# A PSUM tile for each purpose in a kernel of chunked recurrent attention and a mixture of experts

## The chip, the cores and the metric

The kernel runs on one core of one Trainium2 chip. The metric is the device time of one execution in microseconds; the median of the runs counts. The core has a matmul engine (TensorE, in the rows PE, its weight loads PEld), a vector engine (VectorE, DVE), a scalar engine (ScalarE, ACT), a general one (GpSimd, POOL) and a queue for loads and stores (SyncE, SP). Matmul results lie in PSUM, 128 partitions of eight banks of 512 fp32 values.

## The reference

Two stages. The first is a linear attention with decay, over four batches, eight heads, 768 tokens and head size 48; its output, as 3072 rows of 384 values, goes into a mixture of eight experts, of which each row takes one or none.

```python
for t in range(S):                                  # B, H, S, D = 4, 8, 768, 48
    kt, vt, rt = (k[:, :, t], v[:, :, t], r[:, :, t])
    cur = np.einsum('bhd,bhe->bhde', u[None] * kt, vt)
    y[:, :, t] = np.einsum('bhd,bhde->bhe', rt, state + cur)
    state = w[None, :, :, None] * state + np.einsum('bhd,bhe->bhde', kt, vt)
...
skip_score = x @ w_skip                             # x: 3072 x 384
do_compute = skip_score > 0
logits = x[do_compute] @ w_gate                     # 8 experts
e_idx = np.argmax(logits, axis=1)
...
    h = np.maximum(xc[mask] @ w1[e], 0.0)           # 384 -> 1024
    y[mask] = gate_w[mask, None] * (h @ w2[e])      # 1024 -> 384
out[do_compute] = xc + y
```

## The kernel before

**The step loop.** The attention goes in chunks of 64 tokens of two batches: two pairs of batches times twelve chunks are 24 steps. `load_step` brings `dm` (r and k, decay side up) and `vkv` (v, in a block diagonal form whose other blocks are blanked once by `blank`). `prep_r` and `prep_k` multiply r and k by powers of the decay into `rd` and `kd`, `bonus` makes the second half of `rd`. On PE a step n is, in written order: `scores(n+1)` (L467, into `ps_p`), `within(n)` (L517, masked scores `am` times v, into `ps_y`), the turn of the output of step n-1 (L570, into `ps_t`), the turn of k for step n+1 (L445, into `ps_l`), the new state (L491, into the first bank of `ps_s`), in some steps the products of the gate, idle products, and `across(n)` (L533, old state `sblk` times r, into `ps_y`); then ACT copies `ps_y` to `xt` (L544) and SP stores it. DVE masks the scores (L478, L480).

**Idle products.** `warm(k)` multiplies a tile of ones by itself into the second bank of `ps_s`, k times. `NWARM` is 17, at the start; `FILL` says how many stand in a step, and a step that isn't in it has none.

```python
FILL = {0: 3, NSTEP - 1: 4, NSTEP: 3, NT - 3: 2, NT - 2: 3, NT - 1: 4}
```

**Routing.** From step 8 on, generators made by `route` build the expert lists of groups of steps between the steps: small DVE operations, counts of ranks on PE (L663, L664, L673, into `pr`) and list products (L731, L756, into `mine`). `pr` and `mine` are parts of the second bank of `ps_y`. The gate's logits (`gate`, L610) of the last steps are computed step by step. After the first 20 steps are listed (L764 the last product of it), `place` makes the indices and the first `gather` (L129, an indirect DMA on POOL) fetches the first 128 rows for expert 0.

**Transition.** Step 23 contains `begin`: `single` works off expert 0's lists in small pieces (turn L150, `widen` L201, `flip` L213 to L216, `narrow` L223), in turn with the last routes; a string `PLAN` sets the order of the pieces of its two lists.

**Experts 1 to 7.** `expert` computes the hidden values of 232 rows in four quarters, by `up` (L159) into the banks of kind "ph", `rectify` makes `hh` (ACT, L163) and the remainder `hl` (DVE, L164); then `turn_all` turns the rows of the next expert (L150, into the banks of kind "pt", read by L151 and L152); then `down` (L169) computes two sets of rows into the banks of kind "py", `mix` (L174) and `scatter` (L178) end them. Weights come as fp32 (`raw`) and are split in 12 pieces into a high part on ACT (`whi`, L119) and a remainder (`wlo`, L120), every third piece on POOL and the others on DVE.

**Order and waits.** PE, DVE, ACT and POOL work in the order in which the program is written; SP's queue is ordered by a scheduler. Waits follow from the tiles: whoever writes a PSUM tile waits until its earlier readers and writers on other engines are done, whatever part of the tile they touched. The tiles and the rotation of the banks are:

```python
ps_p = psum.tile([P, 2, 512], F32, name="ps_p")
ps_y = psum.tile([P, 2, 512], F32, name="ps_y")
ps_s = psum.tile([P, 2, 512], F32, name="ps_s")
ps_t, ps_l = (psum.tile([P, 512], F32, name=f"ps_{c}") for c in "tl")
...
    "ph": [ps_p[:, 0], ps_s[:, 1], ps_l, ps_s[:, 1]],
    "pt": [ps_s[:, 0], ps_t],
    "py": [ps_p[:, 1], ps_y[:, 0]],
```

## Time and profile before

| | |
|---|---|
| Median of three runs | 312.61 us |
| The three runs | 312.61, 312.81, 305.22 us |
| The profiled execution | 305.04 us |
| Its span, first to last instruction | 303.3 us |
| Mean granted clock of TensorE | 0.971 of full speed |
| Busy | PE 268.8 us, DVE 176.4, ACT 139.6, POOL 143.6 |

The page and the trace are of the profiled execution, so sums are made against 305.04. Times in rows are microseconds from the start of the span. The granted clock is a share of 2.4 GHz: 1.00 is that, 0.50 is 1.2 GHz. In the rows of a timeline, what stands in brackets is how long the engine was idle before the instruction, and what it waited for last.

### The profile page before, as it was taken

Reading aid. Unit: us, or ns where it says so; the run is one execution under the profiler, and the core shown is the slowest. Engines: PE = TensorE matmul, PEld = TensorE weight load, DVE = VectorE, ACT = ScalarE, POOL = GpSimd, SP = SyncE. Lnnn points to the kernel's source line nnn. Section 1 sums busy time; section 2 is a strip of 40 time slices with the busy share of each in tenths; the row PEclk is TensorE's granted clock in tenths of the full one; section 3 lists DMA queues with packets and bytes.
Section 4 is the critical chain, followed back from the end, with each engine's and each line's share of the span. In section 5 each row is a group of like instructions: output and inputs, shape, how many; then the busy total and the mean of one; then the engine's idle time right before and its main releaser. Section 6 shows DMA issues by size and latency. Waiting matters only on the chain.

```text
span 303.3 us, 8820 instructions
## 1 busy us (share of the span) xinstructions
PE 268.8 (89%) x3617; PEld 235.8 (78%) x3617; DVE 176.4 (58%) x382; ACT 139.6 (46%) x317; POOL 143.6 (47%) x154
## 2 busy tenths in 40 slices
PE   7199899999999989876998989799898998989991
PEld 2168778887787767753787979699898998989991
DVE  0978535488555696542554678954827648284310
ACT  1046556574576634421266671633807447182200
POOL 8069545474856544110078888323544434435111
PEclk9879999999999999998999999979999999999997
DMA  7789899999785832294033349915629083100001
GB/s 166 178 285 318 239 266 296 288 294 293 221 219 160 238 88 54 45 317 164 0 94 101 108 147 363 385 66 191 268 77 361 21 302 148 38 4 26 14 20 31
DMA packets 20771, 52.25 MB, mean 172 GB/s; under 512 B 4232, under 2 KB 10891, under 8 KB 20720
## 3 DMA queue, kind: packets, MB, share of 16 engines
q1 hardware_dynamic: 18144, 46.42, 49.1%
q0 software_dynamic: 2048, 5.14, 5.3%
q8 instruction: 31, 0.51, 0.7%
q14 instruction: 20, 0.16, 0.2%
q10 hardware_dynamic: 528, 0.02, 0.1%
HBM read 43.77 MB, written 8.36 MB: 172 GB/s over the span
## 4 chain that ended last, share of the span: by engine, by line
PE 71%; DVE 9%; DMA 7%; issue 5%; ACT 3%; POOL 3%; SPq 0%; POOLq 0%; ACTq 0%; DVEq 0%
PE ps_p L169 10%; PE ps_y L169 10%; PE ps_s L159 9%; PE ps_p L159 5%; PE ps_y L517 4%; PE ps_p L467 4%; PE ps_s L491 4%; PE ps_l L159 4%; PE ps_s L261 3%; PE ps_y L533 3%; PE ps_t L570 3%; DMA xg<-out_dram,gid 2%; DMA dm<-in_dm_dram 2%; PE ps_l L445 2%; DMA raw<-in_w_dram 2%
## 5 line engine op out<-in xcount | busy, mean ns | idle before, releaser
L120 POOL TENSOR_TENSOR wlo<-raw,whi 128x512 fp32r<-128x512 f32 x40 | 53.9, 1352 | 60.4 <-ACT whi L119 43.8
L119 ACT CAST whi<-raw 128x512 fp32r<-128x512 f32 x96 | 54.6, 622 | 0.0
L120 DVE TENSOR_TENSOR wlo<-raw,whi 128x512 fp32r<-128x512 f32 x56 | 49.3, 901 | 3.5 <-ACT whi L119 3.2
L178 POOL DMA_INDIRECT out_dram<-xg,sid x16 | 17.6, 1098 | 39.0 <-DVE xg L174 36.3
L467 PE MATMUL ps_p<-rd,kd 48*64 48x128 f32 x768 | 28.1, 280 | 8.5 <-DVE kd L435 6.8
L435 POOL TENSOR_TENSOR kd<-dm,w_d 112x512 f32<-112x512 f32 x23 | 29.3, 1274 | 7.5 <-DVE pw L345 7.4
L129 POOL DMA_INDIRECT xg<-out_dram,gid x16 | 18.4, 1149 | 27.5 <-DVE sid L777 16.6
L467 PEld LDWEIGHTS ps_p<-rd,kd 48*64 48x64 f32 x768 | 22.1, 137 | 10.8 <-ACT rd L430 7.3
L413 DVE TENSOR_TENSOR rd<-dm,w_d 112x512 f32<-112x512 f32 x24 | 19.1, 801 | 17.3 <-PE ps_y L533 13.6
L159 PE MATMUL ps_s<-x,whi 128*128 128x232 f32 x168 | 28.9, 274 | 0.0
L430 ACT ACTIVATE rd<-rd,uw 112x128 f32<-112x128 f32 x50 | 17.3, 397 | 19.2 <-DVE rd L413 19.0
L159 PEld LDWEIGHTS ps_s<-x,whi 128*128 128x128 f32 x168 | 25.5, 192 | 0.0
L163 ACT ACTIVATE hh<-ps_p 128x464 fp32r<-128x464 f32 x7 | 3.9, 558 | 43.8 <-PE ps_p L159 43.8
L422 POOL TENSOR_TENSOR rd<-rd,uw 112x256 f32<-112x256 f32 x22 | 14.3, 650 | 19.4 <-DVE rd L413 15.7
L159 PE MATMUL ps_s<-x,wlo 128*128 128x232 f32 x84 | 23.2, 277 | 0.0
L517 PE MATMUL ps_y<-vkv,am 128*64 128x96 f32 x384 | 21.4, 253 | 1.8 <-ACT xt L544 1.3
L517 PEld LDWEIGHTS ps_y<-vkv,am 128*64 128x64 f32 x384 | 16.7, 136 | 6.8 <-ACT xt L544 2.8
L478 DVE COPY_PREDICATED am<-below,ps_p 128x512 f32<-128x512 int8 x24 | 17.6, 734 | 5.7 <-PE ps_p L467 4.9
L169 PE MATMUL ps_p<-whi,hh 128*128 128x384 f32 x56 | 20.1, 358 | 0.0
L491 PE MATMUL ps_s<-vkv,kt 128*48 128x96 f32 x352 | 19.6, 253 | 0.0
L169 PE MATMUL ps_p<-wlo,hh 128*128 128x384 f32 x56 | 19.4, 346 | 0.0
L169 PE MATMUL ps_p<-whi,hl 128*128 128x384 f32 x56 | 19.3, 344 | 0.0
(219 smaller groups left out, 620.4 us busy)
## 6 DMA issues: line engine op xcount, KB each, us to landing
raw<-in_w_dram SPq DMA_DIRECT2D x16, 768.0 KB, 7.9
dm<-in_dm_dram SPq DMA_DIRECT2D x24, 448.0 KB, 5.8
raw<-in_w_dram SPq DMA_DIRECT2D x18, 512.0 KB, 5.7
out_dram<-xt SPq DMA_DIRECT2D x56, 96.0 KB, 4.2
vkv<-in_tok_dram SPq DMA_DIRECT2D x48, 96.0 KB, 4.9
raw<-in_w_dram SPq DMA_DIRECT2D x12, 256.0 KB, 6.5
xg<-out_dram,gid POOLq DMA_INDIRECT x16, 3.5
out_dram<-xg,sid POOLq DMA_INDIRECT x16, 2.9
```

What stands on the lines that cost most here:

```text
L119: nc.scalar.copy(hi[:, s], t[:, s])
L120: (eng or nc.vector).tensor_tensor(lo[:, s], t[:, s], hi[:, s].bitcast(F32), ALU.subtract)
L129: ins = nc.gpsimd.indirect_dma_start(out=xg[:m], out_offset=None, in_=out, in_offset=bass.IndirectOffsetOnAxis(ap=gid[:m, q : q + 1], axis=0),
L159: nc.tensor.matmul(ph, w1[a][:, c, fs], x[:, c, b, :], start=(k == 0), stop=(k == 3 * NCC - 1))
L169: nc.tensor.matmul(py, a, b[:, f, :], start=(k == 0), stop=(k == 3 * NFC - 1))
L178: ins = nc.gpsimd.indirect_dma_start(out=out, out_offset=bass.IndirectOffsetOnAxis(ap=sid[:m, q : q + 1], axis=0), in_=xs.pop(q)[:m], in_o ...
L413: nc.vector.tensor_tensor(rd[:, :, :, 0], d, w_d[:, n % NSUB, 0][:, None].to_broadcast([DR, NB, NHP, C]), ALU.mult)
L435: (eng or nc.gpsimd).tensor_tensor(kds[n].rearrange("p b h c -> p b (h c)"), d, w_d[:, n % NSUB, 1].rearrange("p h c -> p (h c)")[:, None, ...
L467: nc.tensor.matmul(ps_p[g * C : (g + 1) * C, a, j * P : (j + 1) * P], kd[h, b, hp, :], rd[h, b, hp].rearrange("p s c -> p (s c)"), start=True,
L478: nc.vector.copy_predicated(shape(am[n % 2]), below, p[:, :, 0])
L491: nc.tensor.matmul(s[a * C : a * C + D, j * 2 * D : (j + 1) * 2 * D], kt[:, j, a, :], v[:, j, a], start=i == 0 and j == 0, stop=True, skip ...
L517: nc.tensor.matmul(ps_y[b * C : (b + 1) * C, a, jj * 2 * D : (jj + 1) * 2 * D], am[n % 2][:, a, j * C : (j + 1) * C], v[:, j, a], start=jj ...
```

## The change

The tile `ps_s` of two banks becomes two tiles of one bank, `ps_s` and `ps_x`; all eight banks stay in use. The state keeps `ps_s`. The idle products, the route's rank counts (`pr`) and list products (`mine`) write `ps_x`; the last ones before expert 0 write `ps_l`. The banks of kind "ph" become `ps_p`, `ps_l`, `ps_x`, `ps_l`. There are 18 idle products fewer: 14 in the steps, one of the six and all three of the three after step 23. DVE blanks one `vkv` tile instead of two, POOL three in front instead of four, and two more in steps 1 and 2.

```diff
@@ -30,7 +30,7 @@
 NT = NPAIR * NSTEP
 CAP = 232
 NXG = 6
-FILL = {0: 3, NSTEP - 1: 4, NSTEP: 3, NT - 3: 2, NT - 2: 3, NT - 1: 4}
+FILL = {0: 2, NSTEP - 1: 2, NSTEP: 1}
 NCC = DM // P
 NFC = F // P
 NJ = 2
@@ -76,8 +76,7 @@
     psum = ctx.enter_context(tc.tile_pool(name="psum", bufs=1, space=PSUM))
     ps_p = psum.tile([P, 2, 512], F32, name="ps_p")
     ps_y = psum.tile([P, 2, 512], F32, name="ps_y")
-    ps_s = psum.tile([P, 2, 512], F32, name="ps_s")
-    ps_t, ps_l = (psum.tile([P, 512], F32, name=f"ps_{c}") for c in "tl")
+    ps_s, ps_x, ps_t, ps_l = (psum.tile([P, 512], F32, name=f"ps_{c}") for c in "sxtl")
 
     ident = cpool.tile([P, P], F32, name="ident")
     make_identity(nc, ident)
@@ -256,9 +255,9 @@
         ones = cpool.tile([P, 512], BF16, name="ones")
         nc.vector.memset(ones, 1.0)
 
-        def warm(k):
+        def warm(k, to=ps_x):
             for _ in range(k):
-                nc.tensor.matmul(ps_s[:, 1], ones[:, :P], ones, start=True, stop=True)
+                nc.tensor.matmul(to, ones[:, :P], ones, start=True, stop=True)
 
         warm(NWARM)
 
@@ -300,9 +299,8 @@
         am = [tab.tile([P, 2, NHP * C], F32, name=f"am{j}") for j in range(2)]
         nc.gpsimd.memset(am[0], 0.0)
         nc.gpsimd.memset(am[1], 0.0)
-        nc.vector.memset(ps_s[:, 0], 0.0)
+        nc.vector.memset(ps_s, 0.0)
         blank(0, nc.vector)
-        blank(1, nc.vector)
 
         def lower(name, op):
             t = tab.tile([P, C], I8, name=name)
@@ -321,7 +319,7 @@
 
         below = lower("below", ALU.is_gt)
         eye = lower("eye", ALU.is_equal)
-        for j in range(2, NVK):
+        for j in range(1, 4):
             blank(j, nc.gpsimd)
 
         w_d = tab.tile([DR, NSUB, 2, NHP, C], F32, name="w_d")
@@ -484,7 +482,7 @@
             i, sub = n % NSTEP, n % NSUB
             if i == NSTEP - 1:
                 return
-            s = ps_s[:DR, 0, : NB * NHP * D]
+            s = ps_s[:DR, : NB * NHP * D]
             v = t.rearrange("p g (j a d) -> p j a g d", j=4, a=2)
             for j in range(4):
                 for a in range(2):
@@ -618,7 +616,7 @@
             seen[0] = n
 
         NV3 = 3
-        mine = ps_y[:, 1, 192 : 192 + NV3 * NSL]
+        mine = ps_x[:, : NV3 * NSL]
         lists = cpool.tile([P, NV3, NJ, E], F32, name="lists")
 
         def route(g0, g1):
@@ -659,7 +657,7 @@
             oh = small("oh", BF16, E)
             nc.vector.tensor_tensor(oh, eq[:, :, :E], bc(m2), ALU.is_equal)
             yield 4 if late else 1
-            pr = ps_y[:, 1, 256:]
+            pr = ps_x[:, 256:]
             nc.tensor.matmul(pr[:, : n * E], tri, oh.rearrange(col), start=True, stop=False, skip_group_check=True)
             nc.tensor.matmul(
                 pr[:, : n * E],
@@ -799,8 +797,8 @@
                 pass
 
         banks = {
-            "ph": [ps_p[:, 0], ps_s[:, 1], ps_l, ps_s[:, 1]],
-            "pt": [ps_s[:, 0], ps_t],
+            "ph": [ps_p[:, 0], ps_l, ps_x, ps_l],
+            "pt": [ps_s, ps_t],
             "py": [ps_p[:, 1], ps_y[:, 0]],
         }
         used = dict.fromkeys(banks, 0)
@@ -892,7 +890,7 @@
             if n == NT - 1:
                 step_route(4)
                 tick(6)
-                warm(6)
+                warm(5, ps_l)
                 vctx.close()
                 scr.append(lctx.enter_context(tc.tile_pool(name="scr", bufs=4, side="right", reuse_waits="tile")))
                 first = begin(0, "vkv")
@@ -904,6 +902,8 @@
                 routes.append([route(ends[n], n), 0, n])
             if 1 <= n < 5:
                 next(setup, None)
+            if n in (1, 2):
+                blank(n + 3, nc.gpsimd)
             if n in RAW0:
                 load_expert(0, RAW0.index(n), 6)
             for j in RAW1.get(n, ()):
@@ -916,7 +916,6 @@
             for _ in range(k):
                 next(first, None)
 
-        warm(3)
         run(1)
         gate(NT - 1)
         for r, *_ in routes:
```

In the changed kernel line numbers are one or two lower. On SP's queue the scheduler now puts the loads of `dm3`, `dm4` and `dm5` each ahead of the `vkv` load of the same step, and spreads the first four pieces of expert 0's weights, which stood close together after `dm4`, over later steps.

First place: DVE at the start of the program, up to the first operation on the decay (`pw`). Before:

```order
L257 MEMSET ones 128x512
L295 MEMSET wg_sb 128x96
L303 MEMSET ps_s 128x512 [waits PE_49]
L281 MEMSET vkv_124 64x384 x2
L281 MEMSET vkv_125 64x384 x2
L339 TENSOR_SCALAR pw<-w_in 112x16 [waits DMAHW1_49]
```

DVE at the same place in the changed kernel:

```order
L256 MEMSET ones 128x512
L294 MEMSET wg_sb 128x96
L302 MEMSET ps_s 128x512
L280 MEMSET vkv_125 64x384 x2
L337 TENSOR_SCALAR pw<-w_in 112x16 [waits DMAHW1_49]
```

The memset of `ps_s` lost its wait for PE, and one of two blanks is gone.

Second place: PE in step 22, from the new state to the products of the last list of the first 22 steps. Before:

```order
L491 MATMUL ps_s<-vkv_128,kt_2139 48x96 x8
L261 LDWEIGHTS ones
L261 MATMUL ps_s<-ones 128x512 [waits Activation_49]
L261 LDWEIGHTS ones
L261 MATMUL ps_s<-ones 128x512
L261 LDWEIGHTS ones
L261 MATMUL ps_s<-ones 128x512
L610 MATMUL ps_t<-wg_sb,xT_2248 128x9 x3
L533 MATMUL ps_y<-sblk_205,rd_1915 64x48 x16
L756 MATMUL ps_y<-vl_2211,ol_2206 128x48 [waits DVE_49,Activation_49]
L756 MATMUL ps_y<-vl_2211,ol_2206 128x48 x3
```

PE at the same place of step 22 in the changed kernel:

```order
L489 MATMUL ps_s<-vkv_129,kt_2135 48x96 x8
L608 MATMUL ps_t<-wg_sb,xT_2242 128x9 [waits Activation_49]
L608 MATMUL ps_t<-wg_sb,xT_2242 128x9 x2
L531 MATMUL ps_y<-sblk_202,rd_1911 64x48 x16
L754 MATMUL ps_x<-vl_2205,ol_2200 128x48 [waits DVE_49]
L754 MATMUL ps_x<-vl_2205,ol_2200 128x48 x3
```

The three idle products went, and with them the wait for ACT that the first one had (for the copy of the state); the gate's first product now has one (for the copy of the turned x). L756, now L754, writes `ps_x` and lost its wait for ACT (for the copy of y); `within` in the next row of its tile waits for ACT now, in place of DVE.

Third place: PE in expert 1, from the last product of `up` over the turn of the next expert's rows to `down`. Before:

```order
L159 MATMUL ps_s<-x_2658,whi_2560 128x232 x2
L159 MATMUL ps_s<-x_2658,wlo_2561 128x232
L150 MATMUL ps_s<-ident,xg_2515 128x128 [waits DMASW4_49,DVE_49]
L150 MATMUL ps_s<-ident,xg_2515 128x128 x2
L150 MATMUL ps_t<-ident,xg_2519 128x104 [waits DMASW5_49]
L150 MATMUL ps_t<-ident,xg_2519 128x104 x2
L169 MATMUL ps_p<-whi_2560,hh_2734 128x384 [waits Activation_49]
L169 MATMUL ps_p<-wlo_2561,hh_2734 128x384
```

PE at the same place of expert 1 in the changed kernel:

```order
L158 MATMUL ps_l<-x_2641,whi_2543 128x232 x2
L158 MATMUL ps_l<-x_2641,wlo_2544 128x232
L149 MATMUL ps_s<-ident,xg_2498 128x128 [waits DMASW4_49]
L149 MATMUL ps_s<-ident,xg_2498 128x128 x2
L149 MATMUL ps_t<-ident,xg_2502 128x104 [waits DMASW5_49]
L149 MATMUL ps_t<-ident,xg_2502 128x104 x2
L168 MATMUL ps_p<-whi_2543,hh_2717 128x384 [waits Activation_49]
L168 MATMUL ps_p<-wlo_2544,hh_2717 128x384
```

The first turn waits for its gather alone; the wait for DVE (`hl` of the last quarter, which read `ps_s`) is gone from it, since that quarter now lies in `ps_l`.

## Rows read from the trace of the kernel before

**Rows 1.** Busy time, share of the span and instructions of each engine.

```profile
PE 268.8 (89%) x3617; PEld 235.8 (78%) x3617; DVE 176.4 (58%) x382; ACT 139.6 (46%) x317; POOL 143.6 (47%) x154
```

**Rows 2.** PE by stretches: us, busy (instructions), granted clock, DMA share, GB/s.

```profile
5.60:12.40 6.80, 1.76 (x8) 1.00 1.01 242
12.50:19.20 6.70, 4.99 (x46) 0.50 0.50 152
19.30:142.10 122.80, 112.37 (x2556) 1.00 0.77 227
142.20:145.50 3.30, 2.97 (x9) 0.50 0.02 5
...
196.80:200.10 3.30, 3.30 (x14) 0.50 0.48 199
```

**Rows 3.** The list of waits: us in total, times, the longest.

```profile
PE ps_s L150 <- DVE hl L164: 7.4, 6, 2.1
...
PE ps_y L663 <- ACT xt L544: 2.6, 4, 0.6
```

**Rows 4.** Timeline of PE at the start: start, us, operation, count, idle before.

```profile
1.52 5.85 PE L261 MATMUL ps_s<-ones 128*128 128x512 bf16 x17 [1.52 <-DVE ones L257]
14.21 1.98 PE L467 MATMUL ps_p<-rd,kd 48*64 48x128 f32 x32 [6.84 <-DVE kd L435]
...
19.78 1.10 PE L467 MATMUL ps_p<-rd,kd 48*64 48x128 f32 x32
```

**Rows 5.** Timeline of DVE at the start.

```profile
7.55 0.48 DVE L303 MEMSET ps_s<- 128x512 f32 x1 [5.98 <-PE ps_s L261]
8.10 1.87 DVE L281 MEMSET vkv<- 64x384 f32 x4
...
12.31 0.69 DVE L413 TENSOR_TENSOR rd<-dm,w_d 112x512 f32<-112x512 f32 x1
```

**Rows 6.** Timeline of SP at the start: the issue of the first `dm`.

```profile
1.25 0.41 SPq L287 DMA_DIRECT2D dm<-in_dm_dram  x1
```

**Rows 7.** The tile `dm`: from issue to landing of its 24 loads.

```profile
DMA to landing us min/median/max: 3.9/5.8/7.6
```

**Rows 8.** Timeline of PE in steps 11 and 20.

```profile
71.79 1.03 PE L261 MATMUL ps_s<-ones 128*128 128x512 bf16 x4
...
117.79 1.07 PE L756 MATMUL ps_y<-vl,ol 128*128 128x48 f32 x8 [0.38 <-ACT xt L544]
```

**Rows 9.** Timeline of PE from step 21 into expert 0.

```profile
123.00 0.59 PE L261 MATMUL ps_s<-ones 128*128 128x512 bf16 x2 [0.63 <-ACT sblk L505]
...
129.76 0.81 PE L261 MATMUL ps_s<-ones 128*128 128x512 bf16 x3 [0.58 <-ACT sblk L505]
130.41 0.73 PE L610 MATMUL ps_t<-wg_sb,xT 128*128 128x9 f32 x6
...
132.35 0.63 PE L756 MATMUL ps_y<-vl,ol 128*128 128x48 f32 x4 [0.60 <-ACT xt L544]
...
140.82 0.55 PE L150 MATMUL ps_s<-ident,xg 128*128 128x128 f32 x3 [1.45 <-DMA xg<-out_dram,gid]
...
143.40 0.99 PE L201 MATMUL ps_p<-whi,xhl 128*128 128x512 f32 x1
...
160.91 0.48 PE L201 MATMUL ps_s<-wlo,xhl 128*104 128x512 f32 x1 [1.22 <-DVE hl L216]
```

**Rows 10.** Timeline of POOL in step 23: the first gather.

```profile
134.09 1.26 POOL L129 DMA_INDIRECT xg<-out_dram,gid  x1 [6.87 <-DMA raw<-in_w_dram]
```

**Rows 11.** Timeline of ACT after the turn of the first gathered rows.

```profile
141.41 0.48 ACT L151 CAST xhl<-ps_s 128x384 fp32r<-128x384 f32 x1 [3.62 <-PE ps_s L150]
```

**Rows 12.** Timeline of POOL around the first expert's `down`.

```profile
175.76 2.51 POOL L120 TENSOR_TENSOR wlo<-raw,whi 128x512 fp32r<-128x512 f32 x2
```

**Rows 13.** Timeline of PE, the first products of `down` of expert 1.

```profile
177.68 0.42 PE L169 MATMUL ps_p<-whi,hh 128*128 128x384 f32 x1
...
178.11 0.34 PE L169 MATMUL ps_p<-whi,hl 128*128 128x384 f32 x1
```

## The prediction

> **What bounds the kernel now.** I read the page's busy line first. TensorE (PE) is busy 89% of the span and no other engine reaches 60% [rows 1], so time can come out of PE's idle stretches, out of products that compute nothing, and out of PE's clock. The split by clock comes next: apart from the first products and the tail, three stretches ran at 0.50, the lower of the two levels (1.2 against 2.4 GHz), at 12.5 to 19.2, 142.2 to 145.5 and 196.8 to 200.1 us; the long loop between them ran at 1.00 [rows 2]. Then the list of waits, for the ones in which PE waits for a reader of a PSUM tile: the expert phase loses 7.4 us in six waits of the token turn (L150) for `hl`, and the loop 2.6 in four waits of L663 for the copy of y [rows 3]. The timelines give their places. The largest single gap is at the start: 17 idle products end at 7.37, and the first scores start at 14.21, 6.84 later [rows 4]. The reader is to see whose fault that is: the vector engine (DVE) waits 5.98 us at L303, a memset of one half of `ps_s`, until idle products in the other half are done [rows 5]. Halves of one tile wait for each other everywhere in this kernel, and that is what the waits below share.
>
> **Reference time.** All terms are taken off the profiled execution, 305.04 us, of which the span is 303.3. It is the low one: the median of the runs is 312.61, 7.6 higher, and two runs of three stand there. No view tells why, so the difference goes into the range, not into the sum.
>
> **The start.** The memset of `ps_s` no longer waits (first order listing) and one of two blanks leaves DVE, half of 1.87 us. What the memset held is DVE's queue: blanks, decay powers, `rd0`, `kd0`; and `kd0` holds PE's first scores. DVE alone could move 5.98 + 0.94 = 6.9 earlier [rows 5], `rd0` from 12.31 to 5.4. What is late next is its load: `dm0` is issued at 1.25 [rows 6], and a `dm` load takes 3.9 to 7.6 us to land, in the median 5.8 [rows 7], so `dm0` lands at 5.2 to 8.9, by the median at 7.05, and the gain is 3.5 to 6.9, by the median 5.3. It is the first large load, which speaks for a shorter landing; I take 5.5. Scores then start at about 8.7, 1.3 after the idle products. If the clock now stays up, the first scores, 1.98 at the lower level against 1.10 later [rows 4], give another 0.9, but the next links are `dm1` and `dm2`, so I count it at nothing (0 to 0.9). Blanks of vkv4 and vkv5 now stand in POOL's queue in steps 1 and 2, ahead of the bonus of `rd5` and `rd6`, which scores want two steps later: half of DVE's 1.87 us for each (an estimate from DVE's row), against two steps of 5.2 us (PE's work from 14.21 to 139.37, 1.45 before 140.82, over 24 steps [rows 4, 9]); nothing. On SP's queue `dm3` to `dm5` move ahead of `vkv3` to `vkv5`, and the weight pieces of expert 0 come later; `dm3` waits there for `kd0`, which comes earlier too. Without that cover a late load costs the start's gain back (a rival below).
>
> **The loop, steps 11 to 20.** The route's products go to `ps_x`, so they no longer wait for the copy of `ps_y`: 0.64 each in steps 11 and 19, two of the four of 2.6 [rows 3], and 0.38 at L756 in step 20 [rows 8]. Step 11 loses two of four idle products, step 12 two of three; one costs 1.03 / 4 = 0.26 [rows 8], four 1.0, but the copy of the turned x or of the logits is wanted right after them, so between 0 and 1.0; I take 0.6. Sum 1.28 + 0.38 + 0.6 = **2.3** (1.7 to 2.7).
>
> **Steps 21 and 22.** No fill any more, and no wait for the copy of the state, which was only the fill's: its tile was the state's. Step 21 gives the wait of 0.63 and 0.43 of products, step 22 goes from 129.76 − 0.58 = 129.18 to the gate at 130.41, 1.23 [rows 9]; the gate itself keeps a wait for the copy of x (second listing), made before that of the state on ACT. Then 0.64 at L663 and 0.60 at L756 [rows 3, 9]. Sum 3.5; the routing chain on DVE runs beside it and is late next, so I take **3.0** (2 to 3.5). The first gather follows L756 through DVE: POOL issues it at 134.09 [rows 10] and its rows come at 140.82, 6.7 us later [rows 9]. It moves with the chain, and it bounds step 23; so the four idle products, one of the last six and 0.64 that vanish there give nothing, and PE's idle time before L150 grows from 1.45 by about 1.5 to 2.
>
> **Transition.** After turning the first tokens PE waited for DVE, for the idle products' tile, and ran three of them before L201 at 143.40. L201 now waits only for the first copy, which ACT ends at 141.41 + 0.48 = 141.89 [rows 9, 11]: 1.5, and 0.3 more as L731 leaves y's tile. **1.8**; if the low half on DVE is late, 0.8. In the second list of expert 0, 1.22 of waiting for `hl` at 160.91 [rows 9] goes with the shared tile: **1.2**.
>
> **Expert phase.** L150 keeps only its wait for the gather (third listing): 7.4 [rows 3]. What is queued behind it is L169, whose third product wants `hl` of the first quarter, done long before; that of the last quarter is wanted six eighths into a stretch, some 3 us later. In expert 1 POOL is late next: its two pieces of `wlo` (8 and 11 of 12) end at 177.0 and 175.76 + 2.51 = 178.3 [rows 12]. Piece 8 holds a part of the third of eight slices of w2, so the eighth product of L169 wants it, products following 0.17 apart, 177.68 + 7 x 0.17 = 178.9 [rows 13], 1.9 after it is there. PE gains 1.22 and this turn's own wait, 1.2 on the mean [rows 3], up to there, so about 0.5 comes back as a wait. With 0.6 more for the five others I take **6.3** (3 to 7.4). The stretch at 0.50 that ends at 200.1 follows the longest of the six, 2.1 us [rows 2, 3]. If it goes, half of 3.3 us is saved at most; **1.2** (0 to 1.7).
>
> **Sum.** 5.5 + 2.3 + 3.0 + 1.8 + 1.2 + 6.3 + 1.2 = 21.3; 305.0 − 21.3 = **283.7**, say 284.
>
> **Rivals.** (a) *The start belongs to the loads.* DMA engines were at 1.01 of their time from 5.6 to 12.4 us and at 0.50 in the slack after it [rows 2]; steps that come sooner ask sooner for `dm1` to `dm5`. If the loop's loads decide, 5.5 falls to about 1 and the time is 288. For it: they ran at 0.77 over the loop. Against: the weights move away from these microseconds.
> (b) *The expert waits only move.* If `wlo` or `hl` stop L169 each time where L150 had stopped, 6.3 and the clock's 1.2 fall to 1 and 0: 290. For it: DVE makes both, and POOL's pieces in expert 1 are tight [rows 12]. Against: L169's first products need older data.
> (c) *Slower: the clock falls in the loop*, as 18 idle products go; PE's first gap, at the end of 17 of them, let it fall to 0.50 [rows 2, 4]. A step's scores took 1.98 at the lower level against 1.10, so a step costs at least 0.9 more, and if all of its 5.2 us went by that ratio, 4.2; I take 2. From 11 steps of 24 at the lower level the gain is gone, and with 15 the time is 314. Against it: steps 1 to 10 and 13 to 20 had no fill and ran at 1.00 [rows 2]. The Trainium skill, "TensorE: Matmul & The Clock Gate", section "What's actually happening", speaks against this change: the throttled state is the default there, and only activity lifts it. By that rule alone each product left out is a risk; rows 2 agree on the gap and show none in the unfilled steps.
> (d) *It does what it says but PE's shorter steps meet DVE*, whose routing work then sets steps 20 to 23: the 3.0 and half of the loop's term go, 288.
>
> **Chances.** The sum 0.58, (a) 0.13, (b) 0.14, (d) 0.10, (c) 0.05. Its own range, by the ends of the terms: start 3.5 to 6.9, loop 1.7 to 2.7, steps 2 to 3.5, transition 0.8 to 2, lists 1.2, experts 3 to 7.4, clock 0 to 1.7, which all together are 12.2 to 25.4, so 279.6 to 292.8. They will not all fall on one side; (a), (b) and (d) lie inside. The runs' own spread of 7.4 can come on top of the sum, 291, and on a rival, 296. I leave out what is beyond 295, and go down to 278 for first scores at full clock as well. 2% of 305 is 6.1, about what a measurement here can tell from no change. Faster 0.93: all but (c) and two rivals at once; within 2%, 0.04, of which (c) with few steps is 0.02; slower 0.03, (c) with 14 steps or more.
>
> **What would show it.** The DVE memset near 1.6 without a wait, scores(0) near 8.7, and scores(1) 5 to 6 us sooner than at 19.78 [rows 4], the later ones with them; no wait of L663 for ACT; no row of PE waiting for ACT's `sblk`; L150 waiting for DMA alone, with the first gather's gap above 2.5 us; L201 within 0.3 of ACT's copy; clock 1.00 from the first scores to the gather, and in place of three low stretches two or one. Wrong would be: scores(2) or (3) waiting for `dm` rows on DVE (a); L169 with waits on POOL or DVE of over 0.8 an expert (b); loop stretches at 0.50 (c); scores waiting for `am` in steps 20 to 23 (d).

## The result

The changed kernel takes 292.17 us in the median of four runs (290.59 to 298.17), the kernel before 309.8 in four (305.22 to 312.81). The ratio is 0.951, with a 95% interval of 0.941 to 0.962. (All ratios here leave out runs over 1.5% above the fastest of their kernel, so they aren't quite those of the medians, and the traces of x1 to x5 below are of such slower runs.) The profiled execution took 290.59 us (span 288.8) against 305.04 (303.3): 14.5 us less; the medians differ by 17.6. Forecast were 284 and a gain of 21.3; the range was 278 to 295. It is faster by less than forecast.

First the page's busy line of the changed kernel, to be held against [rows 1]:

```profile
PE 265.6 (92%) x3599; PEld 234.8 (81%) x3599; DVE 178.7 (62%) x380; ACT 139.9 (48%) x317; POOL 144.6 (50%) x156
```

PE is busy 3.2 us less, somewhat under the price of the 18 idle products that are gone (4.6 at 0.26 each [rows 8]); the rest of the gain is waiting. The list of waits of the changed kernel (us in total, times, the longest) answers to [rows 3]:

```profile
ACT xt L542 <- DMA out_dram<-xt: 8.0, 8, 2.4
PE ps_y L515 <- ACT xt L542: 7.0, 6, 1.8
...
PE ps_s L149 <- DMA xg<-out_dram,gid: 2.7, 1, 2.7
...
PE ps_l L158 <- DVE hl L163: 2.5, 2, 2.2
```

The two waits named in [rows 3] are gone altogether. In their place PE waits 7.0 us in `within` (L515, before L517) for ACT's copy of y; ACT in turn waits 8.0 us for stores, since this copy may not overwrite one that is not stored yet; and in the expert phase 2.5 us at L158 for `hl`.

PE by stretches in the changed kernel (us, busy, granted clock, DMA share, GB/s), against [rows 2]:

```profile
17.60:20.90 3.30, 3.30 (x29) 0.50 0.64 164
21.00:133.50 112.50, 102.16 (x2416) 1.00 0.82 235
133.60:140.40 6.80, 6.56 (x23) 0.50 0.12 48
...
184.80:188.10 3.30, 3.30 (x17) 0.50 0.98 378
```

There are again three stretches at 0.50 before the tail: 3.4 us at the start instead of 6.8, 6.8 in the transition instead of 3.4, and again 3.4 in expert 2.

The timeline of PE at the start, against [rows 4], of DVE, against [rows 5], and of POOL:

```profile
8.13 1.10 PE L465 MATMUL ps_p<-rd,kd 48*64 48x128 f32 x32
...
11.65 1.10 PE L465 MATMUL ps_p<-rd,kd 48*64 48x128 f32 x32 [0.22 <-DVE am L478]
...
17.46 1.51 PE L515 MATMUL ps_y<-vkv,am 128*64 128x96 f32 x16 [1.78 <-ACT xt L542]
...
21.98 1.07 PE L465 MATMUL ps_p<-rd,kd 48*64 48x128 f32 x32
```

```profile
1.68 0.48 DVE L302 MEMSET ps_s<- 128x512 f32 x1
...
5.55 0.69 DVE L411 TENSOR_TENSOR rd<-dm,w_d 112x512 f32<-112x512 f32 x1
...
9.33 0.69 DVE L411 TENSOR_TENSOR rd<-dm,w_d 112x512 f32<-112x512 f32 x1 [1.13 <-DMA dm<-in_dm_dram]
...
15.62 1.93 DVE L411 TENSOR_TENSOR rd<-dm,w_d 112x512 f32<-112x512 f32 x2 [1.31 <-POOL w_d L330]
```

```profile
9.47 1.68 POOL L433 TENSOR_TENSOR kd<-dm,w_d 112x512 f32<-112x512 f32 x1 [2.94 <-DMA dm<-in_dm_dram]
```

The memset starts at 1.68 without a wait, `rd0` at 5.55, and the first scores follow the idle products without a gap, at full clock; scores(1) comes at 11.65, 8.1 us sooner than before. What is late next is the load of `dm1`: DVE waits 1.13 us for it and POOL 2.94. POOL's products and tables follow it without a long pause, and `rd3` on DVE waits 1.31 us for one of these tables (`w_d`, L330). Behind it on ACT lies the copy of y, and behind that PE's L515 at 17.46, after which the clock falls; scores(3) comes at 21.98, and only 5.2 of the 8.1 us are left.

Transition and first gathered rows, against [rows 9]:

```profile
132.79 0.55 PE L149 MATMUL ps_s<-ident,xg 128*128 128x128 f32 x3 [2.72 <-DMA xg<-out_dram,gid]
...
133.91 0.79 PE L200 MATMUL ps_p<-whi,xhl 128*128 128x512 f32 x1 [0.24 <-ACT xhl L150]
```

The gap before the gathered rows is 2.72 us instead of 1.45; L200 follows ACT's copy by 0.05 us.

To see where the time went, I cut each trace at six starts on PE: scores(3), scores(11), scores(20), the first turn of gathered rows, the first `down` product of expert 1, and the end of the last `down` product. The table has the stretches between them in us; experiments are included, each from its profiled execution.

| kernel | scores(3) at | 3 to 11 | 11 to 20 | 20 to turn | turn to `down` | `down` to end | end at |
|---|---|---|---|---|---|---|---|
| before | 27.1 | 36.9 | 42.4 | 34.4 | 36.9 | 119.4 | 297.1 |
| changed | 22.0 | 36.8 | 43.2 | 30.9 | 34.6 | 115.0 | 282.4 |
| changed, on a second chip (x5) | 22.1 | 36.8 | 46.5 | 30.1 | 35.3 | 115.0 | 285.8 |
| three buffers of xt (x1) | 21.7 | 37.0 | 45.6 | 30.4 | 31.8 | 113.4 | 279.8 |
| weights earlier (x2) | 21.3 | 37.5 | 46.4 | 30.7 | 34.8 | 115.0 | 285.8 |
| fourth bank (x3) | 19.9 | 41.1 | 45.9 | 29.1 | 32.2 | 111.5 | 279.6 |
| tables on DVE (x4) | 20.3 | 37.1 | 48.6 | 30.4 | 32.9 | 111.6 | 281.0 |
| old start (x6) | 27.5 | 36.8 | 42.8 | 30.3 | 32.7 | 111.7 | 281.7 |
| idle products back (x7) | 22.5 | 35.7 | 44.8 | 29.6 | 31.8 | 115.1 | 279.6 |
| splits on DVE (x8) | 21.2 | 37.0 | 49.2 | 30.1 | 31.9 | 110.7 | 280.1 |
| fewer weight loads (x9) | 21.9 | 36.1 | 40.7 | 29.8 | 31.7 | 115.0 | 275.3 |
| fewer loads, old start (x10) | 25.6 | 38.2 | 41.3 | 29.0 | 31.7 | 111.7 | 277.5 |
| combination (x11) | 22.4 | 35.2 | 45.2 | 28.4 | 32.3 | 110.6 | 274.2 |
| combination, 14 idle products (x12) | 22.0 | 35.7 | 45.9 | 29.1 | 31.5 | 110.6 | 274.9 |

From the first two lines the gain is 5.2 up to scores(3), 0.1, −0.8, 3.5, 2.3 and 4.4: 14.7. A single execution of the same kernel moves by some us: x5 ran from 284.63 to 296.59 in six runs, and its trace differs from the changed kernel's by 3.3 us between steps 11 and 20 alone. The stretches move too: nine of the traces from changed on leave the expert phase as it is in the changed kernel, and `down` to the end took 115.0 or 115.1 in five of them (changed, x2, x5, x7, x9), 113.4 in x1 and 111.6 or 111.7 in three (x4, x6, x10). So times within 3 us of each other tell nothing here, and a stretch of one trace tells something only where its rows name the wait.

### The profile page after: what moved, and what is told of

The parts are those of the page before. It is cut to its first block, busy times and chain, and to the rows that moved or that the text cites. A ratio compares the mean times of both kernels' runs of the same rounds, so it can differ in the third digit from the quotient of the medians.

```text
span 288.8 us, 8775 instructions
## 1 busy us (share of the span) xinstructions
PE 265.6 (92%) x3599; PEld 234.8 (81%) x3599; DVE 178.7 (62%) x380; ACT 139.9 (48%) x317; POOL 144.6 (50%) x156
## 4 chain that ended last, share of the span: by engine, by line
PE 67%; DMA 16%; POOL 4%; issue 4%; ACT 3%; DVE 3%; SPq 2%; POOLq 0%; ACTq 0%; DVEq 0%
PE ps_l L158 9%; PE ps_p L168 9%; PE ps_y L168 9%; DMA out_dram<-xt 7%; PE ps_y L515 5%; DMA raw<-in_w_dram 5%; PE ps_s L489 4%; PE ps_p L158 4%; PE ps_p L465 4%; PE ps_x L158 3%; PE ps_t L568 3%; PE ps_y L531 2%; DMA xg<-out_dram,gid 2%; PE ps_l L443 2%; DMA dm<-in_dm_dram 2%
## 5 line engine op out<-in xcount | busy, mean ns | idle before, releaser
L119 POOL TENSOR_TENSOR wlo<-raw,whi 128x512 fp32r<-128x512 f32 x40 | 53.6, 1344 | 64.0 <-ACT whi L118 41.1
L119 DVE TENSOR_TENSOR wlo<-raw,whi 128x512 fp32r<-128x512 f32 x56 | 54.5, 992 | 2.3 <-ACT whi L118 2.1
L177 POOL DMA_INDIRECT out_dram<-xg,sid x16 | 17.9, 1122 | 31.9 <-DVE xg L173 28.9
L158 PE MATMUL ps_l<-x,whi 128*128 128x232 f32 x168 | 30.7, 284 | 2.5 <-DVE hl L163 2.5
L433 POOL TENSOR_TENSOR kd<-dm,w_d 112x512 f32<-112x512 f32 x23 | 30.7, 1334 | 3.0 <-DMA dm<-in_dm_dram 2.9
L411 DVE TENSOR_TENSOR rd<-dm,w_d 112x512 f32<-112x512 f32 x24 | 16.8, 702 | 24.3 <-PE ps_y L531 19.8
L158 PEld LDWEIGHTS ps_l<-x,whi 128*128 128x128 f32 x168 | 26.7, 200 | 2.9 <-DVE hl L163 2.9
L515 PE MATMUL ps_y<-vkv,am 128*64 128x96 f32 x384 | 21.9, 257 | 7.1 <-ACT xt L542 7.0
L465 PE MATMUL ps_p<-rd,kd 48*64 48x128 f32 x768 | 27.0, 273 | 1.4 <-issue 1.2
L515 PEld LDWEIGHTS ps_y<-vkv,am 128*64 128x64 f32 x384 | 17.3, 139 | 11.9 <-ACT xt L542 9.7
L465 PEld LDWEIGHTS ps_p<-rd,kd 48*64 48x64 f32 x768 | 21.2, 133 | 3.4 <-issue 2.9
L158 PE MATMUL ps_l<-x,wlo 128*128 128x232 f32 x84 | 23.9, 285 | 0.0
L168 PE MATMUL ps_p<-whi,hh 128*128 128x384 f32 x56 | 19.5, 347 | 0.0
L476 DVE COPY_PREDICATED am<-below,ps_p 128x512 f32<-128x512 int8 x24 | 17.6, 732 | 2.9 <-PE ps_p L465 2.3
L168 PE MATMUL ps_p<-wlo,hh 128*128 128x384 f32 x56 | 18.9, 338 | 0.1
L168 PE MATMUL ps_y<-whi,hh 128*104 128x384 f32 x56 | 18.9, 338 | 0.0
```

The source lines that it names most:

```text
L119: (eng or nc.vector).tensor_tensor(lo[:, s], t[:, s], hi[:, s].bitcast(F32), ALU.subtract)
L158: nc.tensor.matmul(ph, w1[a][:, c, fs], x[:, c, b, :], start=(k == 0), stop=(k == 3 * NCC - 1))
L168: nc.tensor.matmul(py, a, b[:, f, :], start=(k == 0), stop=(k == 3 * NFC - 1))
L177: ins = nc.gpsimd.indirect_dma_start(out=out, out_offset=bass.IndirectOffsetOnAxis(ap=sid[:m, q : q + 1], axis=0), in_=xs.pop(q)[:m], in_o ...
L433: (eng or nc.gpsimd).tensor_tensor(kds[n].rearrange("p b h c -> p b (h c)"), d, w_d[:, n % NSUB, 1].rearrange("p h c -> p (h c)")[:, None, ...
L465: nc.tensor.matmul(ps_p[g * C : (g + 1) * C, a, j * P : (j + 1) * P], kd[h, b, hp, :], rd[h, b, hp].rearrange("p s c -> p (s c)"), start=True,
```

## The experiments

Runs x1 to x4 shared a chip, x5 to x8 a second one, x9 to x12 a third; the kernel before took 306.42, 307.33 and 310.16 us there in the median.

**Why the loop gives nothing: x1, x2, x6, x9, x10.** My first theory was the stores: two buffers are too few. x1 gives a third:

```diff
-            x = wk.tile([P, DM], F32, tag="xt", name=f"xt{n}")
+            x = wk.tile([P, DM], F32, tag="xt", name=f"xt{n}", bufs=3)
```

> The changed kernel with three buffers for the copy of y (xt) instead of two. Theory S (stores): after the change the loop waits for the stores, because the copy of y of a step may not overwrite the copy of two steps before until that is stored; ACT's waits for stores (8.0 us in eight) and PE's waits of L515 for that copy vanish but for the first (7.0 falls to 2 or less), scores(3) to the turn of the first gathered rows (110.8 us in the changed kernel) becomes 106 to 108, the profiled time 286 to 288. Rival T (throughput of the loads): the loop is short of DMA bandwidth as a whole, the wait only changes its name, to dm loads or to weight pieces, and the time stays within 1 us of 290.6.

Measured: 289.1 us in the median (282.49 to 294.67), profile 288.15. The waits of x1 for DMA between 20 and 112 us:

```profile
DVE rd L411 <- DMA vkv<-in_tok_dram: 7.3, 2, 4.0
...
POOL rd L420 <- DMA vkv<-in_tok_dram: 4.6, 1, 4.6
...
ACT xt L542 <- DMA vkv<-in_tok_dram: 0.9, 2, 0.5
```

No wait of ACT for a store is left, but now DVE and POOL wait for loads, and from scores(3) to the turn it is 113.0 us, not 106 to 108 (changed: 110.8, x5: 113.3). The wait changed its name: the theory of the stores falls, and its rival, throughput, fits. (The profiled time fell by 2.4 us, more than that rival allows; the table has this in the transition and the experts, not in the loop.)

x2 brings the weights of expert 0 back to early steps:

```diff
-RAW0 = (2, 5, 8, 11, 14, 17)
+RAW0 = (1, 2, 3, 4, 5, 7)
```

> The changed kernel with the pieces of expert 0's weights in steps 1, 2, 3, 4, 5, 7 instead of 2, 5, 8, 11, 14, 17. If the loss in steps 8 to 20 comes from weight pieces that now share these steps with the stores (in the kernel before, four of the six were loaded by 27 us), the waits of ACT's copy of y for stores move ahead or vanish, POOL's waits for weight pieces go, and the stretch from scores(11) to scores(21) falls from 48.8 us to 45 to 46, while scores(3) to scores(11), 36.8 us, grows by 0 to 2: the time is 287 to 290. If total bytes decide, the sum of both stretches stays within 1 us of 85.5.

Measured: 292.39 us (288.88 to 294.31), ratio 0.950 (0.938 to 0.961). Steps 11 to 20 took 46.4 us and steps 3 to 11 37.5; the two together 83.9, against 83.3 in the control (x5, below) and 80.0 in the changed kernel's first profile. When the weights come makes no difference to be seen. By throughput alone it should have helped, since x2 did load more early, where there was room:

```profile
20.00:40.00 20.00, 18.90 (x459) 1.00 0.94 258
```

The DMA share there is 0.94, against 0.75 in the changed kernel (below) and 0.82 in the control, and steps 11 to 20 got no shorter by it.

x5 is the control and x6 undoes the start alone:

```diff
-        warm(NWARM)
+        warm(NWARM, ps_s)
```

> The changed kernel, unchanged, for comparison on the same chip: a ratio of 0.94 to 0.96 to the kernel before, profile 288 to 293 us.

> The changed kernel with the 17 idle products of the start writing the state's tile again, so that VectorE's memset waits for them as before; all else as changed. Theory T (throughput): scores(3) comes at 26 to 27.5 instead of 22, but between 40 and 100 us the loads and stores are at 0.93 or more of their time and set the pace, so that of the 5 us lost only 1.5 to 3 are left at scores(21) and at the end: the ratio to the kernel before is 0.955 to 0.965. Rival (the start counts in full): 4.5 to 6 us at the end, ratio 0.968 or more.

Measured: control 292.21 us (284.63 to 296.59), ratio 0.934 (0.924 to 0.945); old start 290.92 (289.73 to 296.39), ratio 0.951 (0.944 to 0.958). In the traces the old start has scores(3) at 27.5, 5.4 later than the control: the memset's wait is what held the start. What is left of that later on this run doesn't tell. At scores(20), 107.1, it is 1.7 against the control (105.4), as throughput has it, but 5.2 against the changed kernel's own trace (101.9); at the first turn, 137.4, it is 1.9 or 4.6. The times disagree as well: in the medians nothing is left, while by the ratios, 0.951 against 0.934 on the same chip, the old start is some 5 us longer (the intervals just touch), which is what the rival said. Both ratios are lower than either theory gave.

The DMA engines in the same stretches (us, PE busy, clock, DMA share, GB/s), the kernel before and then the changed one:

```profile
20.00:40.00 20.00, 18.82 (x435) 1.00 0.96 297
40.00:60.00 20.00, 19.51 (x498) 1.00 1.00 280
60.00:80.00 20.00, 19.36 (x430) 1.00 0.95 276
80.00:100.00 20.00, 19.94 (x484) 1.00 0.72 206
```

```profile
20.00:40.00 20.00, 19.59 (x501) 0.98 0.75 214
40.00:60.00 20.00, 18.36 (x457) 1.00 0.94 259
60.00:80.00 20.00, 18.96 (x428) 1.00 0.97 280
80.00:100.00 20.00, 18.76 (x467) 1.00 0.99 279
100.00:120.00 20.00, 17.62 (x433) 1.00 0.45 125
```

Before, the engines moved 297 GB/s at a share of 0.96 from 20 us on, and had slack from 80. Changed, they are at 0.75 from 20 to 40 and at 0.94 to 0.99 until 100: the early slack isn't used, and the engines are full for longer in steps 11 to 20. That `dm` and `vkv` buffers come free only with the steps would explain it; no run shows it. x9 loads only one of the six pieces of expert 0's weights, so that expert 0 computes with other weights, and x10 undoes the start on top:

```diff
-RAW0 = (2, 5, 8, 11, 14, 17)
+RAW0 = (2,)
...
-            nc.scalar.copy(hi[:, s], t[:, s])
-            (eng or nc.vector).tensor_tensor(lo[:, s], t[:, s], hi[:, s].bitcast(F32), ALU.subtract)
+            r = slice(j % 2 * q, (j % 2 + 1) * q) if e == 0 else s
+            nc.scalar.copy(hi[:, s], t[:, r])
+            (eng or nc.vector).tensor_tensor(lo[:, s], t[:, r], hi[:, s].bitcast(F32), ALU.subtract)
```

> The changed kernel with five of the six pieces of expert 0's weights not loaded: all of its twelve splits read the first piece, so expert 0's output is of other weights and 2.6 MB less are moved in steps 5 to 17. Theory T (throughput): 2.6 MB at the 270 GB/s of the stretch 40 to 100 us are 9.7 us of loads; PE's waits of over 0.3 us in the loop for loads and stores (4 to 6 us in the runs so far) fall under 1.5, scores(3) to the turn of the first gathered rows is 105 to 107 us instead of 110 to 116, and the time 4 to 7 us under the changed kernel's. Rival: those waits stay (4 us or more), since they come from the order of the queues and not from bytes, and the time falls by less than 2 us.

> The kernel with five pieces of expert 0's weights left out, and the idle products of the start back in the state's tile. Theory T: with the loads out of the way the start counts in full: against the run with fewer loads the first gathered rows' turn and the end come 4.5 to 6 us later (in the runs with all loads it was 1.9 us at that turn and nothing in the median). Rival: the difference is again under 3 us, so something other than bytes absorbs the start.

Measured: x9 287.78 us (283.53 to 291.04), ratio 0.933 (0.925 to 0.941); x10 290.04 (285.28 to 292.14), ratio 0.936 (0.925 to 0.947). DMA in x9 from 80 to 100 us:

```profile
80.00:100.00 20.00, 19.51 (x520) 1.00 0.72 199
```

Steps 11 to 20 take 40.7 us, the shortest of all; scores(3) to the turn is 106.6, inside the forecast. PE's gaps of over 0.25 us from scores(3) to scores(20) add up to 2.2 us against 4.1 in the changed kernel and 7.5 in the control, so not under the 1.5 forecast, but under the 4 of the rival; the kernel before had 2.3. The time is 7.1 us under the changed kernel's in the profile and 4.4 in the median, on another chip; the ratio, 0.933, isn't under the control's. So bytes do lengthen this stretch: that is what x9 shows, by the stretch and its gaps, not by the time. With fewer bytes x10 is 3.7 later at scores(3) and 5.5 at the turn (134.1 against 128.6), as forecast; at the end it is 2.2, under the forecast, because expert 2 was luckier in x10 (below), which has nothing to do with the start. The ratios, 0.936 and 0.933, don't show the difference, so how much of a start lasts is open here too.

**What set scores(3): x4.** Two tables go from GpSimd to DVE:

```diff
-        grow(2, nc.gpsimd)
+        grow(2, nc.vector)
...
-                grow(3, nc.gpsimd)
+                grow(3, nc.vector)
```

> The changed kernel with two tables of decay powers (grow of parts 2 and 3) made on VectorE instead of GpSimd. Theory: with the memset's wait gone it is GpSimd's chain of kd and these tables (9.5 to 20 us without a pause) that sets scores(3) at 21.98; without the tables (1.03 each) scores(3) comes 1.5 to 2.5 sooner, near 20, and the low clock at 17.5 to 20.9 may go. Of that, all stays if the loop is set by PE, and under 0.5 us if it is set by stores and loads. Rival: the loads dm2 to dm4 set scores(3), which stays within 0.5 us of 22.

Measured: 285.47 us (283.95 to 289.2), ratio 0.929 (0.920 to 0.938). scores(3) came at 20.3, 1.7 sooner, and the low clock at 17.5 didn't occur. That is the number forecast, but the table doesn't bear out the cause: x3, which leaves the tables on GpSimd, has scores(3) at 19.9, and x11 and x12, which have them on DVE, at 22.4 and 22.0. In x4 the wait only moved, to scores(2):

```profile
15.78 1.10 PE L465 MATMUL ps_p<-rd,kd 48*64 48x128 f32 x32 [1.39 <-DVE am L478]
```

DVE, which now makes the tables, masks the scores later. What goes with the early scores(3) is the clock: it stayed at 1.00 before scores(3) in x2, x3 and x4 (19.9 to 21.3) and was at 0.50 for 3.0 to 3.4 us in the other seven with the early start and all loads (21.2 to 22.5). At scores(20) x4 was at 106.0, later than the changed kernel's 101.9 and the control's 105.4, so nothing was left of it; the shorter expert phase (111.6 against 115.0) has nothing to do with the edit.

**Expert phase: x3 and x8.** In the changed kernel the second and the fourth quarter of the hidden values share `ps_l` (before, they shared a bank of `ps_s`). The rows of PE, DVE and POOL around the wait in expert 2:

```profile
184.56 0.59 PE L158 MATMUL ps_l<-x,whi 128*128 128x232 f32 x2 [2.17 <-DVE hl L163]
```

```profile
173.17 4.83 DVE L119 TENSOR_TENSOR wlo<-raw,whi 128x512 fp32r<-128x512 f32 x1
...
181.60 2.35 DVE L119 TENSOR_TENSOR wlo<-raw,whi 128x512 fp32r<-128x512 f32 x2
183.88 0.63 DVE L163 SCALAR_TENSOR_TENSOR hl<-ps_l,hh 128x464 fp32r<-128x464 f32 x1
```

```profile
173.63 3.80 POOL L119 TENSOR_TENSOR wlo<-raw,whi 128x512 fp32r<-128x512 f32 x3
```

PE waits 2.17 us for `hl` of the second quarter, which DVE starts at 183.88. DVE is late: one piece of `wlo` of the usual size took it 4.83 us, from 173.17, just while POOL computed three of its own (173.63 to 177.43), and checks of the logits follow. x3 gives the fourth quarter a bank of its own, x8 takes the remainders off GpSimd:

```diff
-            "ph": [ps_p[:, 0], ps_l, ps_x, ps_l],
+            "ph": [ps_p[:, 0], ps_l, ps_x, ps_y[:, 1]],
```

```diff
-                        split_expert(e, w2pool if e % 2 else wpool, j, NPC, nc.gpsimd if j % 3 == 2 else nc.vector)
+                        split_expert(e, w2pool if e % 2 else wpool, j, NPC, nc.vector)
```

> The changed kernel with a fourth bank for the hidden values (the second bank of y's tile), so that the fourth quarter no longer takes the bank of the second. Theory P (the bank): PE's waits at L158 for hl of the second quarter, 2.17 in expert 2 and 0.33 in expert 1, go, and with the gap the low clock after it (184.8 to 188.2): 2.5 to 4 us less, 286.5 to 288 in the profile. Rival V (VectorE is behind in expert 2, by the checks of the logits that stand there): the wait comes back at the down products (L168) for hl or wlo, 1.5 us or more, and the time stays above 289.

> The changed kernel with the remainders of the weights (wlo) of experts 1 to 7 all made on VectorE, none on GpSimd. Theory L (lock): a piece that takes VectorE 0.67 us took 4.83 while GpSimd ran three of its own back to back (at 173 us), and this is what makes hl late for PE at L158 in expert 2 (2.17 us); without GpSimd's pieces no VectorE piece takes over 1.4, the wait at L158 falls under 0.7 and the time by 1.5 to 4 us. Rival (work): VectorE gets 28 more pieces of 0.7, is late with hl in every expert, and the time grows by 2 us or more.

Measured: x3 286.13 us (283.45 to 288.18), ratio 0.930 (0.920 to 0.940); x8 288.57 (285.61 to 294.45), ratio 0.938 (0.928 to 0.947). From `down` of expert 1 on, the table has 111.5 and 110.7 us in place of 115.0: 3.5 and 4.3 less, and the clock stayed at 1.00 there. The times alone would prove little, since x4, x6 and x10 took 111.6 or 111.7 without either edit; in those three the long piece took 4.12 us and PE waited 0.4. The rows decide. The pieces of `wlo` between 140 and 290 us (ns shortest, median, longest), changed and x8:

```profile
L119 DVE TENSOR_TENSOR wlo<-raw,whi x56: 672/682/4827, 145.8 to 262.3; 128x512 fp32r<-128x512 f32 x56
...
L119 POOL TENSOR_TENSOR wlo<-raw,whi x28: 1274/1306/1779, 154.6 to 263.9; 128x512 fp32r<-128x512 f32 x28
```

```profile
L119 DVE TENSOR_TENSOR wlo<-raw,whi x84: 678/683/742, 148.9 to 260.7; 128x512 fp32r<-128x512 f32 x84
```

84 pieces on DVE, none over 0.742 us, and no wait of PE at L158: the lock theory holds. In x3 DVE is as late as in the changed kernel,

```profile
174.51 4.82 DVE L119 TENSOR_TENSOR wlo<-raw,whi 128x512 fp32r<-128x512 f32 x1
```

yet PE doesn't wait at L158, and what comes back is one wait of 0.6 us at L168 for POOL's `wlo`:

```profile
PE ps_p L168 <- POOL wlo L119: 0.6, 1, 0.6
```

The theory of the bank holds too. Either edit removes the same wait.

**Idle products: x7.** It puts 15 of the 18 back, in the new tile:

```diff
-FILL = {0: 2, NSTEP - 1: 2, NSTEP: 1}
+FILL = {0: 3, NSTEP - 1: 4, NSTEP: 3, NT - 3: 2, NT - 2: 3, NT - 1: 4}
...
-                warm(5, ps_l)
+                warm(6, ps_l)
```

> The changed kernel with the idle products of the steps and of step 23 put back (15 of the 18), in the new tile. Theory: those of steps 11 and 12 cost nothing, since the loads decide there; those of 21 and 22, 0.43 and 0.66, cost 1 us less what VectorE's routing hides: 0 to +1.5 us against the changed kernel on the same chip. Rival (clock): the four of step 23 and the sixth shorten the gap of 2.7 us before the first gathered rows, the clock then stays up after it, and the time falls by 1 to 3 us.

Measured: 289.37 us (287.85 to 294.25), ratio 0.948 (0.940 to 0.955); by time not to be told from the control. The gap before the gathered rows was 1.06 us, the clock stayed at 1.00 around it:

```profile
132.00:140.00 8.00, 7.08 (x42) 1.00 0.36 109
183.00:186.00 3.00, 3.00 (x16) 0.50 1.00 411
```

and turn to `down` took 31.8 us instead of 34.6 and 35.3. But x1, x9 and x10 took 31.7 or 31.8 without these products, their low stretches lying ahead of the turn. So the price of the low clock is plain (31.5 to 31.8 in the five traces with 1.00 after the turn, x1 but for its first 0.1 us, x7, x9, x10 and x12; 34.6 to 35.3 in the three with 6.8 us or more at 0.50 after it, changed, x2 and x5), some 3 us; that the products kept it up in x7 fits the rival, but one trace doesn't show it.

**The best of both: x11 and x12.** x11 has the edits of x3, x4 and x8; x12 also 14 idle products in the last place:

```diff
-                warm(5, ps_l)
+                warm(14, ps_l)
```

> The changed kernel with three of the edits tried: a fourth bank for the hidden values, the decay tables on VectorE, all remainders of the weights on VectorE. If the expert phase's gains (3.5 us from the bank, 2 to 5 from the remainders) are separate, 284 us or less in the median, 8 us under the kernel before's ratio of 0.95: 0.92. If both remove the same wait, as L158 in expert 2 suggests, about 286, ratio 0.93.

> The same with 14 idle products instead of 5 before the turn of the first gathered rows (9 more, 0.22 us each). Theory: PE's gap before the gathered rows, 1 to 3 us, is what lets the clock fall to 0.5 for 3.4 or 6.8 us after it; with 2 us of it filled the clock stays at 1.0 and the transition is 1.5 to 3 us shorter than in the same kernel with 5. Rival: the clock falls all the same, or the products delay the turn: no change or up to 1 us more.

Measured: x11 284.46 us (282.06 to 289.61), ratio 0.922 (0.915 to 0.930), clearly faster than the kernel before; against the changed kernel it is under the 0.951 of the first chip, but its interval meets the control's (0.924 to 0.945), so that gain isn't certain; x12 284.83 (283.0 to 287.77), ratio 0.926 (0.919 to 0.934). The median of x11 is the one forecast for separate gains, but its expert phase, 110.6, is that of x8 alone: the bank adds nothing to it there. In x12 the clock stayed at 1.00 through the transition,

```profile
133.00:140.00 7.00, 6.71 (x41) 1.00 0.20 80
140.00:267.00 127.00, 126.58 (x922) 1.00 0.46 162
```

and turn to `down` is 31.5 against 32.3, 0.8 less instead of 1.5 to 3; scores(20) to the turn is 0.7 longer. The sum is nothing.

## Why the prediction was right and where it fell short

The sign and the mechanism were right: the waits were those of a shared tile, and they went. The sum was 21.3 and the profiles differ by 14.5; that 292.17 still lies in the range is owed to its upper end, which was set for rivals and for the spread of the runs. Term by term:

**The start** (5.5): 5.2 at scores(3), and the closeness is luck. `rd0` started at 5.55, when its operands were ready, so `dm0`, which I had priced, was late by nothing; scores(0) gained 6.1 and scores(1) 8.1 (forecast were 5.5 and 5 to 6), also because the first scores ran at full clock, which I had counted at nothing. Then some 3 us were lost again: the chain behind `dm1`, for which POOL waited 2.94, made PE wait 1.78, and the clock fell after it. That is a part of rival (a), where I looked for it. How much of the lead lasts is open: at scores(20) 4.5 of the 5.2 are left between the first two traces (106.4 and 101.9), and x6 gives 1.7 or 5.2.

**The loop** (2.3): −0.8. This is the step that failed. I took the stretch for PE-bound because its gaps named other reasons, so that a wait taken away would count in full, and read 0.77 as the DMA engines' share of the whole loop [rows 2]; cut in pieces it is 0.96, 1.00, 0.95 and 0.72 before, and 0.75, 0.94, 0.97 and 0.99 changed. The waits of 0.64 vanished and waits for stores and loads took their place: PE's gaps from scores(3) to scores(20) went from 2.3 us to 4.1. In the four traces with the early start, all loads and the clock at 1.00 in steps 11 to 20 (changed, x2, x5, x7) these took 43.2 to 46.5 us, in the six others with the early start and all loads, which ran 3.4 us or more of them at 0.50, 45.2 to 49.2; in the two with the late start 42.4 and 42.8, in the two with fewer bytes 40.7 and 41.3. That bytes lengthen these steps is shown (x9); that they are all of the reason is not, since early loads (x2) gained nothing.

**Steps 20 to 23** (3.0 and 0.4 of the loop's term for L756): 3.5, right. Loads have slack there (a share of 0.45 from 100 us), which fits that PE's waits count in full, and the gap before the gathered rows grew by 1.3, a little less than forecast. Rival (d) didn't come.

**Transition and lists** (1.8 and 1.2): L200 started 1.1 us after the turn instead of 2.6, so 1.5 of 1.8. From there to `down` of expert 1 it is 0.9, the 1.2 less what the longer stretch at 0.50 took. I had forecast the longer gap but given it no price; the traces give it, about 3 us where the clock falls for 6.8 (x7).

**Expert phase** (6.3 and 1.2 for the clock): 4.4. Experts 4 to 6 gave 1.2 us each, as forecast. In expert 2 the wait only moved, from 2.11 at the turn to 2.17 at the fourth quarter, and the low clock stayed with it: rival (b) in one place of six. The two quarters that share a bank were in the diff, and that DVE is late there was in the trace before, in the length of that wait; I had priced GpSimd's own pieces, not that they stop DVE's. Chance is large here: the same phase took 111.6 where DVE's long piece was a little shorter (x4, x6, x10), so 4.4 could as well have been 7.8.

**The clock in the loop**, rival (c): it stayed at 1.00 from 21 to 133.5 us with 14 products fewer. In six experiments (x1, x3, x4, x8, x11, x12) 3.4 to 10.2 us of the loop ran at 0.50, mostly from a gap of PE of 1.5 to 2.5 us on. All but one of these stretches lie between 50 and 105 us, where the DMA engines are near full in the traces above; that they come from the loads and not from the missing products is not shown.

## What to carry to other kernels

A PSUM tile of two banks makes its users wait for each other as if they shared data; one tile for each purpose took such waits away here without a further bank, and they show in the list of waits as pairs of lines that share nothing but the tile's name. Before counting a wait in full, cut the loop into pieces and read the DMA share of each: where it is near 1, another wait can take the place of the one removed, whichever is named for it. And before crediting an edit, look at the same stretch in the runs that leave it alone. When a wait is removed, look for the next use of the same late result, not only for the next wait on the same engine.

## What the runs showed of the hardware

**GpSimd stops VectorE for several instructions in a row.** The same subtraction of 128 x 512 took DVE 0.67 us at the least, 4.83 while POOL ran three of its own without a pause, and at most 0.742 in 84 of them when POOL ran none (x8). The Trainium skill, "SBUF — State Buffer", section "Who interferes with whom", has the rule: a VectorE instruction with two SBUF inputs contends with a GpSimd instruction that reads SBUF, and one blocks the other. The traces agree, and add that VectorE's instruction here ended only after three of GpSimd's. How this falls in expert 2 goes with two lengths of the whole phase: with a piece of 4.83 PE waits 2.17 us and the phase is 115.0, with one of 4.12 it waits 0.4 and the phase is 111.6 (x4, x6, x10).

**A gap of one length did and didn't lower the clock.** After 2.17 us without products the changed kernel ran at 0.50 from 184.8 to 188.2. In x1 the same wait was 2.13 us, and the stretch after it ran at full clock:

```profile
183.66 0.49 PE L158 MATMUL ps_l<-x,whi 128*128 128x232 f32 x2 [2.13 <-DVE hl L163]
```

```profile
184.80:188.20 3.40, 3.40 (x28) 1.00 1.02 422
```

The phase took 113.4 instead of 115.0: the low clock costs 1.6 us there, and its chance belongs to the price of a gap.
